# Three weight loads of a kernel's opening stage tied to later matmuls

## The chip, the cores and the metric

One Trainium2 chip, one NeuronCore. The metric is the device time of one launch in microseconds (us). Every kernel shown was run several times, and one further execution was taken by the hardware profiler. The engines are named as the profile names them: PE (matmul) with PEld (its weight loads into the array), ACT (ScalarE), DVE (VectorE), POOL (GpSimd) and SP (SyncE, which here does nothing but issue DMAs). A name with a q at its end (SPq, PEq) is the engine's sequencer, the part that reads instructions, waits on semaphores and issues DMAs.

## The reference

The first half is a recurrence over 768 time steps for 4 batches of 8 heads, each with a state of 48 x 48. The second is a two-layer network with h - tanh(h) between the layers.

```python
for t in range(S):
    cur = np.einsum('bhd,bhe->bhde', u[None] * kt, vt)
    y[:, :, t] = np.einsum('bhd,bhde->bhe', rt, state + cur)
    state = wt[:, :, :, None] * state + np.einsum('bhd,bhe->bhde', kt, vt)
...
x = y.transpose(0, 2, 1, 3).reshape(B * S, H * D)        # 3072 x 384
h = x @ w_in                                             # 3072 x 2048
out = (h - np.tanh(h)) @ w_out                           # 3072 x 384
```

## The kernel before

**Blocks.** Time is cut into 8 blocks of 384 tokens (4 batches, 2 halves of the sequence each). A block's recurrence is done in chunks of 64 steps. Within a chunk everything is a matmul: scores of keys against queries (`own` for the diagonal, `earlier` for what lies off the diagonal, both through `gram`, whose matmuls are line L488 of the profile), the chunk's addition to the state (`update_half`, L611), and the result from states (`from_states`, L673) and from scores (`from_scores`, L691). The result is the network's input xT, three tiles of 128 rows. Then 16 steps f follow in the main loop, one for each 128 columns of `w_in`: three products into one bank (L837), ACT's copy out of it (L840), the polynomial that stands for h - tanh(h), and the second product (L914, or L961 in later blocks). While one block is in the network, the recurrence of the next is done between its steps.

**The boot.** The first block has nothing to hide behind. `boot` writes its order out by hand: the block's heads go in two halves, h1 and h2. For h1: `own`, transposes of the keys (`turn_1`, L511), `earlier`, `update_half`, then `from_scores` and `from_states`. For h2: `update_half`, `own`, `earlier`, `from_states`, `from_scores`. Between these DVE runs the scans of the decays (L411, L423), the scans of the states (`states_half`, L627), and the masked copies of scores out of PSUM (`own()` and `earlier()`, L496). ACT copies the results out (`result_out`, L725), and small DMAs put the rows that lie in a tile of their own into the gaps of xT (`fill_holes`, L732; three on SP's queue, three on POOL's).

**The weights.** They come as 64-bit numbers and are turned into 32 bits on the chip. One `more_weights` issues one raw load (768 KB, line L249) on SP; `convert` makes three ACT pieces (L262: one writes `w_sb`, two write `up`) and one on DVE (L266) of it. There are 16 raw loads. In the order of their issue I number them raw 1, raw 2 and so on; raw 1 to raw 6 belong to the boot, and the main loop issues one in most of its first steps, each tied to ACT's copy of that step. Five buffers hold raw loads.

**Order.** PE, ACT, DVE and SP run in exactly the written order. SP issues one DMA after another, and a DMA that must wait holds up all that are written behind it. `begin_behind(ins, dma)` adds such a wait: the DMA is not issued before the instruction `ins` has ended. `self.done` is the last matmul that a block has written down so far; `self.opened` is the first matmul of the group that was begun last.

What the boot puts on SP's queue, in order: nine loads of the first block's inputs, raw 1, raw 2, a half of the next block's w, raw 3, three `fill_holes`, raw 4, the other half of w, raw 5, the next block's k, raw 6.

Of the kernel before, what the change touches and what calls it, by code (L numbers as in the profile page):

```python
# [125 lines left out]
def kernel(  # L126
# [12 lines left out]
    nc = tc.nc  # L139
# [106 lines left out]
    def load_weights(n, queue):  # L246
        raw = conv.tile([P, 2 * DM, 2], I32, name="raw", tag="raw")
        src = weights[UNITS[n]].bitcast(I32).rearrange("p (n two) -> p n two", two=2)
        return *UNITS[n], raw, queue.dma_start(out=raw, in_=src)  # L249

    def convert(part, j, raw, _, tiles=1):

        lo, hi = raw[:, :, 0], raw[:, :, 1]
        a = w_sb[:, part, 2 * j:2 * j + 2].rearrange("p f c -> p (f c)").bitcast(I32)
        up = conv.tile([P, 2 * DM], I32, name="up", tag="up", bufs=4)
        low, high = (up.bitcast(t).rearrange("p (n two) -> p n two", two=2)[:, :, i]
                     for i, t in enumerate((U16, F16)))

        def scaled(to, of, scale, bias=0.0):
            return lambda: nc.scalar.activation(out=to, in_=of, func=AF.Copy, scale=scale, bias=bias)  # L262

        return [scaled(a.bitcast(F32), hi.bitcast(F32), HIGH_SCALE), scaled(high, hi.bitcast(F32), SIGN_SCALE),
                scaled(low, lo.bitcast(U32), *LOW)], [
                lambda of=slice(i * 2 * DM // tiles, (i + 1) * 2 * DM // tiles): nc.vector.scalar_tensor_tensor(  # L266
                    out=a[:, of], in0=a[:, of], scalar=3, in1=up[:, of], op0=ALU.logical_shift_left,
                    op1=ALU.bitwise_or) for i in range(tiles)]
# [45 lines left out]
    class Block:  # L314
# [186 lines left out]
        def own(self, ps, p0, **fill):  # L501
            return self.masked(ps, "k", "r", masks["diagonal"], p0, **fill)

        def earlier(self, ps, p0, **fill):
            return self.masked(ps, "post", "pre", masks["above"], p0, **fill)
# [89 lines left out]

        def update_half(self, pair, p0):

            self.opened = None
            self.by_column = [t[:, 0:D * NCH].rearrange("d (e c) -> d e c", c=NCH) for t in pair]
            for x in range(UP):  # L600
                if x:
                    nc.tensor.drain().then_inc(fence, 1)
                    fences.append(None)
                    nc.tensor.wait_ge(fence, len(fences))
                for c in range(0, NCH, 2):
                    for h in range(2):
                        for par in range(2):
                            p = (x + par) % UP
                            toks = slice(64 * par, 64 * par + 64)
                            e0 = (p0 + p) * D2 + h * D  # L610
                            self.done = nc.tensor.matmul(self.by_column[p][64 * h:64 * h + 64, :, (c + par + 1) % NCH],  # L611
                                             lhsT=self.ks[toks, p0 + p, c // 2, 64 * h:64 * h + 64],
                                             rhs=self.v[toks, c // 2, e0:e0 + D], start=True, stop=True)
                            self.opened = self.opened or self.done

        def totals_by_column(self, p0):

# [449 lines left out]
    def more_weights(queue):  # L1067
        raws.append(load_weights(more_weights.n, queue))
        more_weights.n += 1
        return raws[-1][-1]  # L1070
# [3 lines left out]
    def begin_behind(ins, dma):  # L1074
        tc.add_manual_dep(dma.ins, ins.ins.name, mybir.DependencyInfo(
            mybir.DependencyClass.Sync, mybir.DependencyReason.DATA))

    def run(ops):
        for op in ops:
            op()  # L1080
# [13 lines left out]
    def boot(ps, pair, blk, later):  # L1094
        h1, h2 = HALVES
        blk.tiles["w"] = states0
        for name, p0, n in (("w", h1 + 1, 1), ("w", h1, 1), ("k", h1, UP), ("r", h1, UP), ("w", h2, UP)):
            blk.load(name, p0, n)
        blk.load_v(h1, UP)
        blk.load("k", h2, UP)  # L1100
        blk.load_v(h2, UP)
        blk.load("r", h2, UP)
        more_weights(nc.sync)

        both = (h1, h1 + 1), (h2, h2 + 1)
        blk.behind(h1 + 1, 1)
        blk.behind(h1, 1)
        blk.take_whole(h1, UP)
        blk.totals_by_column(h1)
        nc.scalar.copy(out=later_ident, in_=ident)  # L1110
        blk.before(h1, UP)
        blk.times_behind(h1, UP)
        blk.times_u(h1, UP)
        own = blk.own(ps, h1, spare=92, ahead=5, late=6)
        blk.turn_1(ps, h1)
        blk.times_before(h1, UP)
        earlier = blk.earlier(ps, h1)
        blk.behind(h2, UP)
        blk.take_whole(h2, UP)
        first_a, first_b = convert(*raws.pop(0), tiles=2)  # L1120
        own()
        blk.turn_2(h1)
        blk.totals_by_column(h2)
        blk.update_half(pair, h1)
        begin_behind(blk.opened, more_weights(nc.sync))
        later.load("w", UP, UP)
        blk.times_behind(h2, UP)
        blk.times_u(h2, UP)
        blk.turn_1(ps, h2)
        blk.turn_2(h2)  # L1130
        earlier()
        blk.results(ps, halved=True)
        blk.result("from_scores", both[0])
        run(blk.states_half(h1))
        blk.result("from_states", both[0], True)
        blk.before(h2, UP)
        blk.update_half(pair, h2)
        begin_behind(blk.opened, more_weights(nc.sync))
        blk.times_before(h2, UP)
        own = blk.own(ps, h2)  # L1140
        run(first_a[:1])
        blk.result_out((3,), nc.scalar.copy)
        blk.result_out((2,))
        earlier = blk.earlier(ps, h2)
        onwards = blk.states_half(h2)
        own()
        run(first_a[1:])
        blk.fill_holes([nc.sync, nc.gpsimd])
        more_weights(nc.sync)
        later.load("w", 0, UP)  # L1150
        second_a, second_b = convert(*raws.pop(0))
        third_a, third_b = convert(*raws.pop(0))
        run(second_a)
        more_weights(nc.sync)
        blk.results(ps, halved=True)
        blk.result("from_states", both[1])
        earlier(1, 1)
        earlier(0, 1)
        for p in reversed(both[1]):
            blk.result("from_scores", (p,), True, more=True)  # L1160
        blk.result_out((1,), nc.scalar.copy)
        later.load("k")
        more_weights(nc.sync)
        run(onwards)
        run(first_b[:1])
        blk.result_out((0,), nc.vector.tensor_copy)
        run(first_b[1:])
        run(third_a[:2])
        run(second_b)
        blk.held(0, NPAIR)  # L1170
        return [(third_a[2], third_b)]
# [6 lines left out]
    with tc.tile_pool(name="ps_boot", bufs=1, space=PSUM) as ps_boot:  # L1178
        pieces = boot(Turns([scratch(ps_boot)] + ps_a.both), [hp] + acc, blocks[0], blocks[1])
# [227 lines left out]
```

## Time and profile before

| | |
|---|---|
| median of 3 runs | 555.3 us |
| lowest, highest | 553.42, 555.8 us |
| the profiled execution's own time | 555.92 us |
| its span in the trace | 554.1 us |
| PE busy | 539.7 us, 97% of the span |
| DVE busy | 459.7 us, 83% |
| ACT busy | 405.0 us, 73% |

Times in the trace count from the first instruction; 1.8 us of the profiled execution lie outside the span. "Idle before" in a row is the time in which the engine did nothing ahead of that instruction, followed by what released it. "Issue" in the chain of waits is time in which an engine waited for nothing that the profile can show. In the DMA view, "q1" is SP's queue, and "instruction" rows are the queues through which engines get their own code.

### The profile page before, as it was taken

The page shows a single profiled execution, that of the slowest core. Times are in us where ns is not written, and L with a number is a line of the kernel's source. Part 1 is how long each engine was busy: PE and PEld are TensorE (multiplying, and loading weights), DVE is VectorE, ACT ScalarE, POOL GpSimd, SP SyncE. Part 2 cuts the span into 40 slices and gives each one's busy share as a digit, 9 for nine tenths or more (in the row PEclk, how much of TensorE's full clock was granted, in tenths as well). Part 3 has the DMA queues.
Part 4 walks back from the last instruction along what each step waited for, and adds up shares of the span by engine and source line. Part 5 has one row for each costly group of instructions (what it writes and reads, how often), then busy time and mean ns, then how long its engine had stood idle before and what let it go on. Part 6 is the DMA issues. An engine that isn't in the chain of part 4 may idle for free.

```text
span 554.1 us, 14163 instructions
## 1 busy us (share of the span) xinstructions
PE 539.7 (97%) x5727; PEld 405.1 (73%) x5727; DVE 459.7 (83%) x943; ACT 405.0 (73%) x814; POOL 5.3 (1%) x33
## 2 busy tenths in 40 slices
PE   8599999999999999999999999999999999999996
PEld 5565556678777787777778787777877787787874
DVE  7679999999988989888997889969797897557563
ACT  4589997798667886588766886588865886666561
POOL 1100000000000000000000000000000000000000
PEclk9789999999999999999999999999999999999999
DMA  8878654244302442237211532126232320100101
GB/s 274 281 258 317 206 178 126 72 122 95 117 13 85 101 117 84 69 79 143 98 54 44 144 116 64 50 88 157 61 93 62 80 65 3 54 1 0 44 2 46
DMA packets 53462, 56.31 MB, mean 102 GB/s; under 512 B 21520, under 2 KB 51344, under 8 KB 53392
## 3 DMA queue, kind: packets, MB, share of 16 engines
q1 hardware_dynamic: 53008, 55.18, 33.6%
q8 instruction: 46, 0.75, 0.6%
q14 instruction: 24, 0.20, 0.1%
q10 hardware_dynamic: 288, 0.10, 0.1%
q0 software_dynamic: 96, 0.07, 0.1%
HBM read 44.73 MB, written 4.72 MB: 89 GB/s over the span
## 4 chain that ended last, share of the span: by engine, by line
PE 90%; ACT 4%; issue 2%; DMA 1%; DVE 1%; PEld 0%; SPq 0%; PEldq 0%; DVEq 0%
PE hp L837 43%; PE acc L961 26%; PE att L961 6%; PE acc L914 4%; PE att L488 2%; ACT up L262 2%; PE att L691 2%; PE att L673 2%; PE acc L939 2%; PE att L569 1%; DMA states<-in_wT 1%; ACT w_sb L262 1%; ACT qa L869 1%; DVE scores L496 0%; ACT h L840 0%
## 5 line engine op out<-in xcount | busy, mean ns | idle before, releaser
L837 PE MATMUL hp<-xT,w_sb 128*128 128x384 f32 x750 | 265.5, 490 | 0.4 <-ACT h L840 0.4
L837 PEld LDWEIGHTS hp<-xT,w_sb 128*128 128x128 f32 x750 | 134.9, 192 | 72.3 <-ACT h L840 1.0
L840 ACT ACTIVATE h<-hp 128x384 f32<-128x384 f32 x125 | 61.5, 492 | 101.5 <-PE hp L837 101.4
L961 PE MATMUL acc<-forms,g 128*128 128x128 f32 x954 | 133.7, 276 | 0.5
L961 PEld LDWEIGHTS acc<-forms,g 128*128 128x128 f32 x954 | 121.6, 192 | 10.2 <-issue 1.2
L843 DVE SCALAR_TENSOR_TENSOR h<-h,s 128x384 f32<-128x384 f32 x128 | 70.9, 554 | 52.3 <-ACT s L858 52.1
L884 DVE TENSOR_TENSOR g<-g 128x256 f32<-128x256 f32 x265 | 103.6, 421 | 7.9 <-PE acc L961 7.0
L859 ACT ACTIVATE qa<-s,shift 128x384 f32<-128x384 f32 x113 | 69.8, 618 | 3.7
L861 ACT ACTIVATE junk<-s,shift 128x384 bf16<-128x384 f32 x113 | 68.0, 602 | 0.0
L843 DVE SCALAR_TENSOR_TENSOR g<-qa,h 128x384 f32<-128x384 f32 x112 | 61.8, 552 | 1.9 <-DVE h L843 0.5
L858 ACT ACTIVATE s<-h 128x384 f32<-128x384 f32 x113 | 59.3, 525 | 3.5
L961 PEld LDWEIGHTS acc<-w_sb,g 128*128 128x128 f32 x318 | 46.7, 191 | 9.7 <-ACT sums L929 0.3
L961 PE MATMUL acc<-w_sb,g 128*128 128x128 f32 x318 | 53.1, 276 | 0.1
L961 PE MATMUL att<-w_sb,g 128*128 128x128 f32 x212 | 35.5, 275 | 0.0
L961 PEld LDWEIGHTS att<-w_sb,g 128*128 128x128 f32 x212 | 31.1, 192 | 5.3
L996 DVE TENSOR_TENSOR sums<-sums 128x256 f32<-128x256 f32 x84 | 33.1, 410 | 1.7 <-ACT sums L973 1.4
L914 PE MATMUL acc<-w_sb,sums 128*128 128x384 f32 x96 | 33.9, 489 | 0.1
L262 ACT ACTIVATE up<-raw 128x768 f16<-128x768 f32 (+1 forms) x32 | 33.2, 1075 | 0.0
L914 PEld LDWEIGHTS acc<-w_sb,sums 128*128 128x128 f32 x96 | 17.8, 190 | 12.1 <-DVE sums L843 0.3
L411 DVE TENSOR_TENSOR_SCAN pre<-w,start 128x780 f32<-128x780 f32 x14 | 25.0, 1783 | 0.5
L423 DVE TENSOR_TENSOR_SCAN post<-w,seed 128x780 f32<-128x780 f32 x14 | 24.9, 1776 | 0.0
L861 ACT ACTIVATION_READ_ACCUMULATOR junk<-s,shift 128x1 f32 x113 | 21.3, 189 | 0.0
(115 smaller groups left out, 523.8 us busy)
## 6 DMA issues: line engine op xcount, KB each, us to landing
raw<-in_weights SPq DMA_DIRECT2D x16, 768.0 KB, 4.9
k<-in_kT SPq DMA_DIRECT2D x7, 768.0 KB, 4.4
r<-in_rT SPq DMA_DIRECT2D x7, 768.0 KB, 4.5
w<-in_wT SPq DMA_DIRECT2D x6, 780.0 KB, 4.6
v_sb<-in_v SPq DMA_DIRECT2D x7, 576.0 KB, 3.8
k<-in_tokens SPq DMA_DIRECT2D x7, 576.0 KB, 3.9
r<-in_tokens SPq DMA_DIRECT2D x7, 576.0 KB, 5.0
out_y<-sums SPq DMA_DIRECT2D x18, 128.0 KB, 1.9
```

The costliest lines, as they stand in the source:

```text
L262: return lambda: nc.scalar.activation(out=to, in_=of, func=AF.Copy, scale=scale, bias=bias)
L411: return nc.vector.tensor_tensor_scan(out=self.tile("pre")[:, cols], data0=self.tile("w")[:, cols], data1=start[:, 0:n * NCH * LP], initia ...
L837: nc.tensor.matmul(hp, lhsT=w_in_sb[:, f, kc, :], rhs=xT[kc], start=(kc == KC - 1), stop=(kc == 0))
L840: return h, nc.scalar.activation(out=h, in_=hp, func=AF.Copy, scale=1.0 / UPSCALE)
L843: return lambda: nc.vector.scalar_tensor_tensor(out=out, in0=in0, scalar=scalar, in1=in1, op0=op0, op1=ALU.mult)
L858: nc.scalar.activation(out=s, in_=h, func=AF.Square)
L859: nc.scalar.activation(out=qa, in_=s, func=AF.Square, bias=shift[:, 4:5])
L861: nc.scalar.activation(out=junk[:, 0:NB], in_=s, func=AF.Relu, bias=shift[:, 5:6], accum_out=excess[:, at:at + 1])
L884: return lambda: nc.vector.tensor_tensor(out=G[:, to:to + 2], in0=two(G, g_at(q, a0), g_at(q, a1)), in1=two(G, g_at(q, b0), g_at(q, b1)), ...
L914: nc.tensor.matmul(acc, lhsT=g[:, j * P:(j + 1) * P], rhs=w_out_sb[:, f, :], start=(f == self.first), stop=(f == NF - 1))
L961: nc.tensor.matmul(to, lhsT=G[:, g_at(q, a), :], rhs=rhs, start=start, stop=stop, skip_group_check=True)
L996: ops.append(lambda op=op, at=at: nc.vector.tensor_tensor(out=at[0], in0=at[1], in1=at[2], op=OPS[op]))
```

## The change

Raw 2 and raw 3 no longer wait for the first matmul of an `update_half` but for the last one. Raw 4, which waited for no matmul, now waits for the last matmul of the second half's off-diagonal scores. The bookkeeping of first matmuls in `update_half` goes. No instruction is added or taken away on any engine and none changes its place; three DMAs have other waits.

```diff
@@ update_half
-            self.opened = None
             self.by_column = [...]
...
                             self.done = nc.tensor.matmul(...)
-                            self.opened = self.opened or self.done
@@ boot
         blk.update_half(pair, h1)
-        begin_behind(blk.opened, more_weights(nc.sync))
+        begin_behind(blk.done, more_weights(nc.sync))
         later.load("w", UP, UP)
...
         blk.update_half(pair, h2)
-        begin_behind(blk.opened, more_weights(nc.sync))
+        begin_behind(blk.done, more_weights(nc.sync))
...
         earlier = blk.earlier(ps, h2)
+        scored = blk.done
         onwards = blk.states_half(h2)
         own()
         run(first_a[1:])
         blk.fill_holes([nc.sync, nc.gpsimd])
-        more_weights(nc.sync)
+        begin_behind(scored, more_weights(nc.sync))
         later.load("w", 0, UP)
```

## The prediction

> **What bounds the kernel now.** I read the page first, then the chain of waits over the boot's end, then SP's queue, the DMA packets in short stretches, and the stretches' busy times. From the page:
>
> ```profile
> PE 539.7 (97%) x5727; PEld 405.1 (73%) x5727; DVE 459.7 (83%) x943; ACT 405.0 (73%) x814; POOL 5.3 (1%) x33
> q8 instruction: 46, 0.75, 0.6%
> ```
>
> PE is busy nearly all the time, so the little it loses is worth asking for. The chain of waits shows where the boot loses it (start, length, what):
>
> ```profile
> 16.64 1.95 issue
> 18.59 0.13 PEld hp L611
> 20.03 2.15 PE att L488 x79
> 22.18 3.02 issue
> 25.20 0.75 PE att L488 x17
> 26.04 1.06 DVE scores L496 x2
> ...
> 28.99 4.15 PE hp L837 x6
> ```
>
> Twice PE waits for nothing visible, 1.95 us at the start of the second `update_half` and 3.02 us in the middle of the second `earlier`. The middle of a group has no wait of the program. Queue q8 gives a reading: 46 packets in 0.75 MB are 16 KB each, and PE's 2 x 5727 instructions over 46 are 249 a packet. So q8 is PE's code, in blocks of about 250 instructions. The stretches (busy us and instructions of PE, then of PEld, then of the others; further on the granted clock and the DMAs' busy share) bear it out:
>
> ```profile
> 12.42:18.50 6.08, 3.87 (x143) 3.15 (x135) 6.01 (x10) 4.57 (x9) 0.90 (x2) 1.00 0.66 241
> 18.55:25.00 6.45, 3.48 (x126) 3.19 (x127) 2.68 (x4) 4.26 (x5) 0.63 (x2) 0.57 0.83 259
> 16.04:19.45 3.41, 1.49 (x70) 1.24 (x66) 2.77 (x3) 2.71 (x6) 1.58 (x3) 1.00 0.40 138
> ```
>
> Between the stalls lie 126 + 127 = 253 instructions, one block; one block back from the first stall is about 12.4 us. Both stalls are PE waiting for its next code block. SP's queue and the DMA view say why the code was late. First SP's issues (start, length; the row from 5.72 is raw 1 with raw 2 merged in), then the code packets in the stretches 16.0 to 16.3, 22.8 to 22.9 and 28.8 to 28.9, then landings (us from issue) of raw 1, raw 2, raw 3, w, two fills on SP, raw 4 and raw 6:
>
> ```profile
> 5.72 7.17 SPq L249 DMA_DIRECT2D raw<-in_weights  x2
> ...
> 12.55 0.34 SPq L249 DMA_DIRECT2D raw<-in_weights  x1
> 12.94 0.43 SPq L363 DMA_DIRECT2D w<-in_wT  x1
> 18.88 0.33 SPq L249 DMA_DIRECT2D raw<-in_weights  x1
> 19.31 1.89 SPq L732 DMA_DIRECT2D xT<-late  x3
> 21.24 0.58 SPq L249 DMA_DIRECT2D raw<-in_weights  x1
> 24.21 0.48 SPq L249 DMA_DIRECT2D raw<-in_weights  x1
> ```
>
> ```profile
> q8 instruction: 1, 0.02, 19.4%
> q8 instruction: 1, 0.02, 58.3%
> q8 instruction: 1, 0.02, 62.2%
> ...
> raw<-in_weights SPq DMA_DIRECT2D x1, 768.0 KB, 9.5
> raw<-in_weights SPq DMA_DIRECT2D x1, 768.0 KB, 4.5
> raw<-in_weights SPq DMA_DIRECT2D x1, 768.0 KB, 5.0
> w<-in_wT SPq DMA_DIRECT2D x1, 390.0 KB, 6.3
> xT<-late SPq DMA_DIRECT2D x2, 24.0 KB, 5.3
> raw<-in_weights SPq DMA_DIRECT2D x1, 768.0 KB, 5.5
> raw<-in_weights SPq DMA_DIRECT2D x1, 768.0 KB, 9.4
> ```
>
> The first code packet begins after 16.0 and lasts 0.194 x 16 x 0.3 = 0.93 us; PE goes on at 18.59, about 1.4 us after it ends. The second begins after 22.8 and PE goes on at 25.20: again 0.93 and 1.4. If PE asks for a block when it enters the one before (at about 12.4 and at 18.59), the two requests waited almost 4 us. In both cases a 768 KB raw load left within 0.3 us of the request (raw 2 at 12.55, raw 3 at 18.88), and the code packet came shortly before that load landed: raw 2 lands at 12.55 + 4.5 = 17.05, raw 3 at 23.88, each about 0.9 us after the packet's start. My reading: the code stood behind the raw load that had just got in ahead of it.
>
> **The change, part by part.** It moves three issues and what SP holds behind them; on PE, ACT and DVE the order is the same. I follow the boot from 12.4 us.
>
> *Raw 2*, tied to the last matmul of the first update. What that adds is read from the second update: raw 3 left at 18.88, after its first matmul, and the chain's next row begins at 20.03, so the last matmul ends 1.15 us later. Raw 2 leaves at 12.55 + 1.15 = 13.7, w behind it at 14.1. Ahead of PE's request of 12.4 is then only raw 1, which landed at 5.72 + 9.5 = 15.2. With the same 0.9 us before the landing, the code packet starts by 14.3 and PE has its block by 14.3 + 0.93 + 1.4 = 16.6. It needs it at 16.64. So the first stall goes: 1.95 us, or, if the packet starts only when raw 1 has landed, 1.0. Raw 2's delay is hidden: it lands by 13.7 + 4.5 = 18.2, and ACT begins on it at 20.05 (row below).
>
> *Raw 3*, tied to the last matmul of the second update. That update now runs from 16.64 to 18.1 (1.44 us as before), and raw 3 leaves at 18.2, even earlier than its 18.88. PE's request for the block after falls at 16.64, 1.5 us ahead of it. Ahead of the request are raw 2 (lands 18.2) and w (14.1 + 6.3 = 20.4). If the packet goes in 0.9 us ahead of one or the other, it starts between 17.3 and 19.5, and PE has its code between 19.6 and 21.8; I take the middle, 20.7, as no row says which.
>
> PE and DVE then go on as follows:
>
> ```profile
> 9.43 1.08 PE L488 MATMUL att<-r,k 48*64 48x64 f32 x48
> 17.93 0.96 DVE L430 TENSOR_TENSOR pre<-r,pre 128x768 f32<-128x768 f32 x1
> 20.05 0.89 ACT L262 ACTIVATE w_sb<-raw 128x768 f32<-128x768 f32 x1
> 20.15 0.76 DVE L627 TENSOR_TENSOR_SCAN first_states<-hp,first_totals 128x288 f32<-128x288 f32 x1 [1.26 <-PE hp L611]
> 21.47 1.02 DVE L496 COPY_PREDICATED scores<-mask_all,att 128x768 f32<-128x768 uint8 x1
> 28.41 0.96 ACT L725 COPY xT<-att 48x384 f32<-48x384 f32 x2 [5.60 <-PE att L691]
> 30.19 1.06 ACT L262 ACTIVATE up<-raw 128x768 f16<-128x768 f32 x1
> 33.17 0.49 ACT L840 ACTIVATE h<-hp 128x384 f32<-128x384 f32 x1 [1.92 <-PE hp L837]
> 34.48 0.90 ACT L262 ACTIVATE w_sb<-raw 128x768 f32<-128x768 f32 x1
> 36.89 2.10 PE L837 MATMUL hp<-xT,w_sb 128*128 128x384 f32 x6
> 41.87 0.92 ACT L262 ACTIVATE w_sb<-raw 128x768 f32<-128x768 f32 x1
> ```
>
> `own` takes 1.08 us, 18.1 to 19.2. `earlier` may start then (DVE's pre is ready at 17.93 + 0.96 = 18.89, whatever PE does). Its first 31 matmuls (79 in the chain's row less the 48 of `own`) end at 19.9, and the code comes at 20.7: a stall of 0.8 us (0 to 1.9) in place of 3.02. `earlier` ends at 21.1. DVE meanwhile starts its two scans at 18.9 instead of 20.15; they and the first masked copy took until 21.47 + 1.02 = 22.49, so now until 21.2 or 21.3. Here DVE becomes what is late next. `from_states` writes the bank that this copy reads and starts at 21.3 instead of after 25.2. The second pair of copies (1.06) ends at 22.4, `from_states` too (48 matmuls, 1.08). `from_scores` ends at 23.5 against 28.99. That is 5.5 us.
>
> The first product hp took 4.15 us at half clock and takes 1.93 at full clock (36.89 and 2.10 with its last matmul's tail). It would end at 25.4, but xT must be copied first (ACT's 0.96 from the middle of `from_scores`, DVE's last copy about 1 us from its end), so 25.3 to 25.5, against 33.14. ACT has 31.25 - 28.41 = 2.84 us of work ahead of h: from 23.0 to 25.8. So h of step 0 starts at 25.9 at best instead of 33.17: 7.3 us. From this I take 0.6 for the fills: SP's three leave at 18.5 to 20.4 behind raw 3, and at 5.3 us the last are there at 25, not at 23.5. **Sum 6.7 us.** From there ACT and PE are both almost gapless, and the main loop moves forward as a whole.
>
> *Raw 4*, tied to the end of `earlier`, at 21.1. Before it left at 21.24, so it is no later, but on its queue wait the other w, raw 5, k and raw 6. ACT needs raw 4 at 34.48 - 6.7 = 27.8; it lands at 21.1 + 5.5 = 26.6. Raw 6 left at 24.21 and lands after 9.4 us; moved with raw 4 it is there at 33.5, due at 41.87 - 6.7 = 35.2. Raw 4's cover is 1.2 us, raw 6's 1.7. If `earlier` ends at 22.2, the upper bound, raw 4's is 0.1, and beyond that every us costs one. PE's block after that is asked for ahead of raw 4.
>
> *The clock.* In the stretch 16.04 to 19.45 PE was busy 1.49 of 3.41 us, and the clock fell to one half right after (0.57 in the row from 18.55) and stayed there through hp. With the first stall gone this stretch is full. The stretch after holds 0.8 + 0.2 us of gaps ahead of `from_states`, up to 1.9 with the bounds, so more work than the one that lost the clock. If the clock falls there, hp runs at 4.15 and its end moves to 27.5, that of step 1 by up to 2 more: the gain is 6.7 - 2 = 4.7 us. The Trainium skill, TensorE: Matmul & The Clock Gate (Part 1: The HAM clock gate), has the clock halved after an idle window of about 3.4 us; by that rule a stretch with work in it would keep it, and only the 6.7 stands. The trace disagrees in degree: 1.49 us of work did not keep it.
>
> So the profiled execution goes from 555.92 to 549.2, and the median, 0.6 lower, from 555.3 to 548.6; I say **549.0**.
>
> **The rivals.** *Half clock*, above: 4.7 us, 550.6. For it speaks that the clock falls on stretches only half empty; against it the first stall's going.
>
> *The code isn't held by the raw loads.* The Trainium skill, DMA: Bandwidth & Descriptors (Queues, rings and completion order), has each DMA engine take turns between queues packet by packet; then a code block would wait for one data packet, not for a load, and reordering loads would move nothing. In rows: the packet at 28.8 to 28.9 went out while raw 6 (lands 33.6) was still queued, so a queue does not have to be empty. Then the second stall stays and at most the first one's 1.95 goes: 553.4 to 555.3, no measurable difference. Against it: two waits of almost 4 us that end 0.9 us ahead of a raw load's landing.
>
> *Loads too late.* With compute earlier by 6.7, the loads of raw 4 to raw 6, w, k and the loop's own raw loads crowd into one stretch, all behind raw 4's new wait. It decides from the point where raw 4 lands after 27.8 and raw 6 after 35.2. For a loss, raw 6 must land past 41.87, at least 17.7 us after an issue at 24.1 and nearly twice its 9.4. If the wait holds SP that long, 3 to 4 us are lost: 559. Nothing in the rows shows such a landing.
>
> **How the numbers follow.** Full clock 0.50, half clock 0.27, code not held by the loads 0.13, loads too late 0.10. Measurement can tell about 0.5%, 2.8 us, from no change; 552.5 is the line. So faster 0.77, same 0.13, slower 0.10. The gaining cases reach from 547.5 (h at its best, 7.3 us, and 0.5 of spread) to 552; the range goes on to 555.5 to hold most of the third case.
>
> **What would show it.** In the profile after: the two issue waits (1.95 and 3.02) gone and at most some 1 us left in `earlier`; code packets near 14 and 18 us; raw 2 at 13.7, raw 3 near 18.2, raw 4 near 21; `from_scores` over near 23.5; h of step 0 near 26; no new wait of ACT for raw. I am wrong if the stalls stay with raw 2 and raw 3 behind the requests, or if ACT's idle time ahead of L262 grows.

## The result, and the profile after

| | before | after |
|---|---|---|
| median of 22 runs each | 554.73 us | 551.25 us |
| lowest, highest | 549.31, 556.25 us | 549.6, 552.58 us |
| the profiled execution's own time | 555.92 us | 551.86 us |
| its span in the trace | 554.1 us | 550.1 us |

The ratio after to before is 0.9942, with a 95% interval of 0.9927 to 0.9958. The change makes the kernel 3.5 us faster by the medians and 4.06 us by the two profiled executions. The prediction had 549.0, so it forecast 6.3 us. The lowest execution of the kernel before, 549.31, lies below all of the kernel after; "What stays open" comes back to it.

The page of the kernel after. PE is still the engine that is busy nearly all the time:

```profile
span 550.1 us, 14164 instructions
PE 536.6 (98%) x5727; PEld 403.5 (73%) x5727; DVE 459.4 (84%) x943; ACT 403.9 (73%) x814; POOL 5.2 (1%) x33
```

The chain of waits of the kernel after over the boot's end (start, length, what):

```profile
17.65 0.97 DVE pre L430
18.62 0.14 issue
18.75 0.69 PE att L488 x31
19.44 2.85 issue
22.29 0.75 PE att L488 x17
...
23.12 1.06 DVE scores L496 x2
...
24.54 1.53 PE att L689 x48
26.08 3.11 PE hp L835 x6
```

The reader is to see two things. The stall of 1.95 us at the second `update_half` is gone: the chain runs through DVE's `pre` into `earlier` instead. The stall in the middle of `earlier` is still there, behind the same 31 matmuls as predicted, and it is 2.85 us long where it was 3.02.

SP's queue in the kernel after (start, length of each group of issues). The first row is raw 1 with raw 2 merged in; it ends at 13.73, so raw 2 itself left at 13.4. The rows from 17.59 and 23.06 are raw 3 and raw 4:

```profile
5.66 8.07 SPq L249 DMA_DIRECT2D raw<-in_weights  x2
13.78 1.30 SPq L363 DMA_DIRECT2D w<-in_wT  x1
17.59 0.33 SPq L249 DMA_DIRECT2D raw<-in_weights  x1
18.07 2.02 SPq L730 DMA_DIRECT2D xT<-late  x3
23.06 0.33 SPq L249 DMA_DIRECT2D raw<-in_weights  x1
```

The code packets in the DMA view of the kernel after, first in the stretch 13.7 to 13.9, then in 19.8 to 19.9 (packets, MB, busy share of 16 engines):

```profile
q8 instruction: 1, 0.02, 29.0%
q8 instruction: 1, 0.02, 64.4%
```

The first block of code now begins to come at 13.8 instead of 16.3, though raw 2 left 0.4 us before it. The second comes at 19.8 and lasts 0.644 x 16 x 0.1 = 1.03 us; PE goes on at 22.29, again 1.4 us after its end. PE entered the block before it at about 16.2, so from entry to packet it is 3.6 us.

The stretches of the kernel after (PE's, PEld's, DVE's, ACT's, POOL's busy us, then granted clock, DMA share, GB/s):

```profile
17.76:21.17 3.41, 1.18 (x66) 0.94 (x56) 3.07 (x4) 3.41 (x5) 1.15 (x3) 1.00 0.84 265
21.17:24.58 3.41, 2.02 (x69) 1.84 (x69) 1.46 (x5) 1.33 (x2) 0.13 (x2) 0.50 0.45 112
24.58:27.99 3.41, 3.41 (x51) 2.45 (x52) 2.11 (x5) 2.46 (x4) 0.00 (x0) 0.50 0.91 341
27.99:31.40 3.41, 3.41 (x12) 2.03 (x11) 2.11 (x5) 2.53 (x5) 0.00 (x0) 1.00 1.00 391
```

The clock still falls to one half right behind the stretch with the stall. It stays there for two stretches of 3.41 us, from 21.17 to 28.0; before, it was four of them, from 19.45 to 33.1. And ACT's row for h of step 0 in the kernel after:

```profile
29.21 0.49 ACT L838 ACTIVATE h<-hp 128x384 f32<-128x384 f32 x1 [0.88 <-PE hp L835]
```

It began at 33.17 before: 3.96 us earlier. The span is 4.0 us shorter, so the main loop moved forward as a whole and nothing was given back later.

### The profile page after: what moved, and what is told of

Same layout as the page of the kernel before. It is cut to its first block, busy times and chain, and to the rows that moved or that the text cites. A ratio compares the mean times of both kernels' runs of the same rounds, so it can differ in the third digit from the quotient of the medians.

```text
span 550.1 us, 14164 instructions
## 1 busy us (share of the span) xinstructions
PE 536.6 (98%) x5727; PEld 403.5 (73%) x5727; DVE 459.4 (84%) x943; ACT 403.9 (73%) x814; POOL 5.2 (1%) x33
## 4 chain that ended last, share of the span: by engine, by line
PE 90%; ACT 4%; DVE 2%; issue 1%; DMA 1%; SPq 0%; DVEq 0%
PE hp L835 43%; PE acc L959 26%; PE att L959 6%; PE acc L912 4%; ACT up L262 2%; PE att L488 2%; PE att L689 2%; PE att L671 2%; PE acc L937 2%; PE att L569 2%; DMA r<-in_rT 1%; ACT w_sb L262 1%; ACT qa L867 1%; ACT h L838 0%; DVE pre L430 0%
## 5 line engine op out<-in xcount | busy, mean ns | idle before, releaser
L859 ACT ACTIVATION_READ_ACCUMULATOR junk<-s,shift 128x1 f32 x113 | 21.1, 187 | 0.0
```

The source lines that it names most:

```text
L859: nc.scalar.activation(out=junk[:, 0:NB], in_=s, func=AF.Relu, bias=shift[:, 5:6], accum_out=excess[:, at:at + 1])
```

## The experiments

The theory by which the prediction stood, the queue: a code block waits behind the raw loads that are queued when PE asks for it, so the right order of loads removes both stalls. The first rival: the code isn't held by loads at all. The second, formed after the first four runs: a code block has a time of its own that no order of loads shortens (the floor), and a load that gets ahead adds to it. Ratios are against the kernel before on the same chip, with 95% intervals.

**Raw 2 alone.** Only the first of the three edits, made to the kernel before:

```diff
         blk.update_half(pair, h1)
-        begin_behind(blk.opened, more_weights(nc.sync))
+        begin_behind(blk.done, more_weights(nc.sync))
```

> Only raw 2 is moved to the last matmul of the first update; raw 3 and raw 4 leave as in the kernel before. Theory A (a code block stands behind the loads queued when PE asks for it) and theory B (a code block waits as long as the DMA engines have any loads to do, also loads issued after the request): the first stall (1.95 us) goes in both. PE then asks for the next block at 16.2, with raw 2 and w under way and raw 3 leaving at about 16.5, so the second stall stays at 2.8 to 3.5 us in both. Time about 1.9 us below before plus up to 1.5 if the clock also keeps its pace longer: 551 to 553. Theory C (the loads do not hold the code): both stalls as before, 554.7.

Measured: median 553.56 (549.02 to 555.08), ratio 0.9985 [0.9958, 1.0012]. Its profiled execution, 550.66, was the second fastest of twelve and so not a typical one. In it the first stall is gone and the second is 1.18 us, by its chain of waits:

```profile
18.81 0.69 PE att L488 x31
19.49 1.18 issue
20.68 0.75 PE att L488 x17
...
24.47 3.46 PE hp L837 x6
```

So raw 2's edit does take the first stall away, which speaks against the first rival. The medians show no gain that is clear of noise. Ten of the twelve executions took 552.38 us or more; where they lost what this one kept, no trace shows. The second stall is what both theories of the expectation had wrong, at 2.8 to 3.5 us: raw 3 left at 16.65, 0.4 us behind PE's entry at about 16.3, and the code packet still came at 18.33 and not near 20. And the DMA engines weren't idle meanwhile (the DMA share is the last number but one):

```profile
16.83:20.24 3.41, 2.04 (x108) 1.73 (x104) 3.38 (x5) 3.36 (x6) 1.57 (x3) 1.00 0.99 356
```

**Raw 3 and raw 4 alone.** The other two edits, made to the kernel before (raw 2 stays tied to the first matmul):

```diff
         blk.update_half(pair, h2)
-        begin_behind(blk.opened, more_weights(nc.sync))
+        begin_behind(blk.done, more_weights(nc.sync))
...
-        more_weights(nc.sync)
+        begin_behind(scored, more_weights(nc.sync))
```

> Only raw 3 and raw 4 are moved, raw 2 leaves as before. A and B: the first stall stays at 1.95 us; PE asks for the next block at 18.6, when raw 2 and w have landed or nearly so and raw 3 has not left (it goes at 20), so the code packet comes by 19.5 and the second stall is 0 to 0.5 us in place of 3.02. Time about 2.5 to 3 us below before: 551.5 to 552.5. C: both stalls stay, raw 4 leaves at 26, time 554.7 or a little above.

Measured: 552.71 (550.61 to 553.83), ratio 0.9969 [0.994, 0.9997]. Its chain of waits:

```profile
16.47 1.92 issue
18.40 0.13 PEld hp L611
...
19.62 1.75 PE att L488 x79
21.38 1.35 issue
22.73 0.75 PE att L488 x17
...
26.52 4.00 PE hp L837 x6
```

The first stall stays, as it should. The second is not gone, as expected at 0 to 0.5 us, but more than halved, 1.35 us. PE entered the block at 18.40 and raw 3 left only at 19.68; the code packet came at 20.2. Something other than a raw load took those 1.8 us: the DMA engines were busy for 0.18 of them.

**Raw 3 far later.** Raw 3 behind the fills and tied to `earlier`, with raw 4 right behind it, to keep it away from the second code block altogether:

```diff
         blk.update_half(pair, h2)
-        begin_behind(blk.done, more_weights(nc.sync))
...
         begin_behind(scored, more_weights(nc.sync))
+        more_weights(nc.sync)
```

> The changed kernel with raw 3 issued behind the fills, tied to the end of the off-diagonal scores, with raw 4 right behind it. In the changed kernel PE asks for the second block at 16.2, raw 2 and w are queued, raw 3 leaves at 17.59, and the code packet starts at 19.84. A: the request is older than raw 3, so nothing changes: packet at 19.5 to 19.9, stall 2.5 to 2.9 us, time as the changed kernel, 3.5 below before. B: the packet goes in when w's data are through, at 18.5 to 18.9, stall 1.5 to 1.9 us, time 1 us below the changed kernel (4.5 below before), unless raw 3 is then late for ACT.

Measured: 551.29 (550.62 to 551.8), ratio 0.9948 [0.9926, 0.997]. The code packet came at 18.45, the stall is 1.19 us, the clock stays at 1.0 and hp takes 2.29 us; but raw 3, issued at 21.36, is now what ACT waits for. Its waits and ACT's row:

```profile
ACT w_sb L262 <- DMA raw<-in_weights: 2.5, 2, 1.7
```

```profile
27.73 0.49 ACT L838 ACTIVATE h<-hp 128x384 f32<-128x384 f32 x1
```

What PE gained was lost to the load: h at 27.73, and no better median than the changed kernel's.

**The half of w later.** The changed kernel with the first half of w moved from behind raw 2 to behind raw 4, so that only raw 2 is on its way when PE asks for the second block:

```diff
-        later.load("w", UP, UP)
...
         begin_behind(scored, more_weights(nc.sync))
+        later.load("w", UP, UP)
         later.load("w", 0, UP)
```

> The changed kernel with the first half of the next block's w issued beside the second half, behind raw 4, instead of right behind raw 2. Ahead of PE's request of 16.2 is then only raw 2, whose data end at about 17.3, and raw 3 leaves at 17.6. A: packet at 17.0 to 17.4, second stall 0 to 0.4 us. B: the same if the gap between raw 2's end and raw 3's first data at 18.4 lets it in, packet at 17.3 to 18, stall 0.2 to 1. Both: time 2 to 2.8 us below the changed kernel, that is 5.5 to 6.3 below before. C: stall 2.85 us as in the changed kernel, no difference from it.

Measured: 550.16 (548.78 to 551.62), ratio 0.9929 [0.9903, 0.9954]. PE's waits, the row of hp and ACT's row of h in its trace:

```profile
PE att L488 <- issue: 0.9, 1, 0.9
PE hp L835 <- DMA xT<-late: 0.6, 1, 0.6
```

```profile
23.93 2.17 PE L835 MATMUL hp<-xT,w_sb 128*128 128x384 f32 x6 [0.57 <-DMA xT<-late]
26.14 0.49 ACT L838 ACTIVATE h<-hp 128x384 f32<-128x384 f32 x1 [0.19 <-PE hp L835]
```

This is the chain that the prediction drew: a stall of 0.9 us in `earlier`, full clock, h at 26.1, its own time 549.12. Between 17.6 and 18.2 the DMA engines moved nothing (0.1% by the DMA view) and the code packet still came only at 18.23. With only raw 2 ahead, the queue theory would have had the code there by 17.4.

**All loads late.** To measure the code's own time, raw 2 goes behind the second `update_half`, raw 3 and raw 4 behind `earlier`, w behind both:

```diff
         blk.update_half(pair, h1)
-        begin_behind(blk.done, more_weights(nc.sync))
-        later.load("w", UP, UP)
...
         begin_behind(scored, more_weights(nc.sync))
+        more_weights(nc.sync)
+        later.load("w", UP, UP)
```

> A probe for the code's latency, not for speed: raw 2 only behind the second update (17.6), raw 3 and raw 4 behind the off-diagonal scores, w behind them, so that the DMA engines have nothing to do from about 14 to 18.5, and PE asks for the second block at 16.2 to 16.4. R: packet 1.9 us after that, at 18.1 to 18.4, stall 0.9 to 1.3 although nothing was queued. B (a block waits only as long as there are loads): packet at about 17.0, no stall. In both ACT waits for raw 2 from about 20 to 22.5, so h of the first step starts at about 28 to 29 and the time is near the changed kernel's or up to 2 us above.

Measured: 552.39 (550.9 to 553.31), ratio 0.9949 [0.9934, 0.9964], with ACT waiting 2.8 us for a raw load. What it was run for, first a stretch with its DMA share, then the code packet in 18.1 to 18.3, then PE's waits:

```profile
14.00:17.60 3.60, 3.20 (x154) 2.80 (x156) 3.57 (x7) 2.90 (x6) 0.24 (x1) 1.00 0.01 3
```

```profile
q8 instruction: 1, 0.02, 42.3%
```

```profile
PE att L488 <- issue: 1.5, 1, 1.5
```

The DMA engines had stood all but still (share 0.01) for over two us when PE entered the block at about 16.3, and the packet came only at 18.17. So about 1.9 us lie between entry and packet with nothing in the way. The packet took 1.35 us in this trace; with the 0.9 that it takes in most, and some 1.4 until PE goes on, the sum is 4.2 us. PE runs through the block in 3.0 to 3.1 us (16.2 to 19.3 in the kernel after, of which 0.5 is a wait for DVE's `pre`). No order of loads tried here brought this stall below 0.86 us. The queue theory falls in this part.

But 1.9 us is what this block shows, not a time that every block needs. At the block before it, which PE enters at about 12.4, the packet came 0.7 us after the entry with raw 2 alone (at 13.16) and 1.5 us after it with all loads late (at 13.9), and at the block behind it 1.1 us after PE went on with the half of w later (20.47 to 21.60). So the floor is measured for this block alone, and why it differs from its neighbours stays open.

**Raw 2 and raw 3 without raw 4.** The changed kernel without the third edit:

```diff
-        begin_behind(scored, more_weights(nc.sync))
+        more_weights(nc.sync)
```

> The changed kernel without its third edit: raw 4 leaves right behind the fills again. First stall gone, second as in the changed kernel (about 2.9 us, packet at 19.8), since raw 4 would leave at about 20.1, after that packet. Theory D (the tie of raw 4 is needed to keep the code ahead of it): a longer second stall, 3.5 us or more, and 0.5 to 1 us above the changed kernel. Theory E (the tie of raw 4 matters for nothing): time equal to the changed kernel, ratio to before 0.993 to 0.996.

Measured: 551.39 (549.84 to 553.33), ratio 0.9942 [0.9922, 0.9963], the same as with it. The third edit makes no difference that these runs can measure. Up to raw 4 this kernel orders everything as the changed one does, yet in its profiled execution raw 3 left at 18.00, the packet came at 18.4, and the stall was 0.86 us, the shortest of all:

```profile
20.70 0.47 PE L488 MATMUL att<-pre,post 48*64 48x64 f32 x17 [0.86 <-issue]
```

The same order can go either way.

**Raw 3 behind `own`.** Raw 3 tied to the last matmul of the second `own`, some 1.2 us later:

```diff
-        begin_behind(blk.done, more_weights(nc.sync))
         blk.times_before(h2, UP)
         own = blk.own(ps, h2)
+        begin_behind(blk.done, more_weights(nc.sync))
```

> The changed kernel with raw 3 tied to the last matmul of the second half's own scores, about 1 us later than to the update's last. Theory R (race with a floor): a code packet starts at the earliest about 1.9 us after PE has entered the block before, and a load whose data reach the engines by then goes first; raw 3 at 17.59 was in time for that in the changed kernel (packet 19.84) and is not at 18.7. Then packet at 18.2 to 18.5, stall 0.9 to 1.3 us in place of 2.85, and raw 3 lands at about 23.5, in time for ACT at 24: time 1 to 2.5 us below the changed kernel, 5 to 6 below before, with the half-clock windows rarer. Theory A (the block stands behind raw 2 and w, which were queued at its request): packet still near 19.8, stall 2.5 to 2.9, no gain on the changed kernel.

Measured: 551.39 (550.18 to 551.66), ratio 0.9931 [0.9911, 0.9952]. In the trace the stall is 1.48 us and the packet is at 18.95, half a us later than expected. The clock is at one half from 21.06 to 27.89, and hp takes 3.51 us. h is at 28.71, only half a us ahead of the changed kernel's.

**Both of these.** The half of w later and raw 3 behind `own`, the two edits above together:

> raw 3 behind the own scores and also w beside its other half behind raw 4. R: the floor stays, packet at 18.2 to 18.5, stall 0.9 to 1.3, the same as with raw 3 moved alone; time the same as that or 0.5 us above, since raw 5 is later by a w. A: with only raw 2 ahead the packet comes at 17.0 to 17.4, stall 0 to 0.3, 1 us below raw 3 moved alone.

Measured: 550.11 (548.91 to 551.45), ratio 0.9911 [0.9889, 0.9934], the lowest of all kernels here, though by less than the noise. Its profiled execution (551.45, its slowest) had a stall of 1.48 us and half clock over hp, 4.18 us.

**Sixteen more instructions.** The changed kernel with eight more spare matmuls (with their weight loads) at the start of the boot. If the stall stands at the border of a code block it must move back by eight matmuls; if it belongs to the step, it must not:

```diff
-        own = blk.own(ps, h1, spare=92, ahead=5, late=6)
+        own = blk.own(ps, h1, spare=100, ahead=5, late=6)
```

> The changed kernel with 8 more of the tiny matmuls that PE does at the start (16 more instructions ahead of everything else). If the second stall is a border between code blocks (theory R), it comes exactly 16 instructions, 8 matmuls, earlier in the off-diagonal scores: the chain shows L488 x23 before and x25 after it instead of x31 and x17 (some 23 to 25 each; the trace may miss a record). Time within 0.3 us of the changed kernel. If the stall belongs to a place in the program (a wait that the profile doesn't show), it stays at x31 and x17.

Measured: 550.99 (548.86 to 553.22), ratio 0.9929 [0.9899, 0.9959]. Its chain of waits:

```profile
18.86 0.57 PE att L488 x23
19.43 2.94 issue
22.37 0.90 PE att L488 x25
```

The stall stands after 23 matmuls of `earlier` instead of 31 and has its old length. It belongs to the instruction count. That was argued in the prediction from packet sizes; here it is shown. The packet in this trace began at 19.0, 0.9 us ahead of the changed kernel's, but took 2.05 us instead of 0.9 to 1.0. That the loads beside it stretched it is likely, not shown.

**The fills ahead of raw 3.** The changed kernel with raw 3, tied to `own`, put behind SP's three fills; and the same with the half of w later:

```diff
-        begin_behind(blk.done, more_weights(nc.sync))
         blk.times_before(h2, UP)
         own = blk.own(ps, h2)
+        owned = blk.done
...
         blk.fill_holes([nc.sync, nc.gpsimd])
+        begin_behind(owned, more_weights(nc.sync))
```

> The changed kernel with raw 3 behind SP's fills and behind the own scores, at about 20. R: code packet at 18.2 to 18.4, stall 1.1 to 1.5; the fills are not behind raw 3 any more; raw 3 lands at about 24.5, so ACT waits for it 0.3 to 0.8 us. Time 0 to 1 us below the changed kernel. If what is left is the half clock after the stall and not the loads, time follows the number of half-clock windows: 549.5 to 550 with one or none, 551.5 with three.

> The same with w beside its other half behind raw 4. R: stall 1.1 to 1.5 as well; raw 3 lands at 24 to 24.5, raw 4 and raw 5 behind it in time. Time as the kernel with w late and raw 3 at 17.7 (550.2) or up to 1 us below, 549 to 550.2, about 1 us below the changed kernel.

Measured: 551.03 (549.99 to 551.79), ratio 0.9927 [0.9903, 0.9951]; and with w later 550.53 (550.11 to 550.75), ratio 0.9918 [0.9889, 0.9947]. The chain of waits of the first:

```profile
19.57 1.46 issue
21.02 0.51 PE att L488 x17
...
24.54 4.12 PE hp L835 x6
```

and its stretch with half clock:

```profile
21.66:28.48 6.82, 6.55 (x96) 4.41 (x92) 4.39 (x10) 3.85 (x6) 0.11 (x2) 0.50 0.95 357
```

The packet came at 18.7 and raw 3 left at 20.75. The stall is half as long, and hp one us longer than in the changed kernel. Of the 1.39 us that the stall gives, 0.53 reach h (28.68 against 29.21). In the second kernel the stall is 0.93 us, and ACT waits 1.9 us for a raw load that left at 20.2.

**The changed kernel once more**, unchanged, to see its stall in a second profiled execution:

> The changed kernel as it is, one more look. Theory R (a race): the same program can win or lose the race between raw 3 and the code packet from one execution to the next. So either packet at 18.2 to 18.6 with a second stall of 1.1 to 1.6 us (won), or packet at 19.6 to 20 and 2.7 to 3.0 us (lost); in both the first stall stays away, and the time is 549.5 to 552.6. Theory A: always packet near 19.8 and 2.9 us.

Measured: one time, 552.64. The kernel before ran once beside it and took 548.67 at a granted clock of 1.0, 4 us less. One execution of each says nothing of the medians, but this is the shortest execution on record here, so the kernel before can run without its loss. The changed kernel's chain of waits:

```profile
18.83 0.69 PE att L488 x31
19.52 2.85 issue
22.37 0.76 PE att L488 x17
...
26.16 3.66 PE hp L835 x6
```

Raw 3 left at 17.85, the packet came at 19.86, and the stall is 2.85 us as in the first trace. With the kernel without the third edit, whose order is the same up to there, that is two late packets in three traces.

## Why the prediction was right, and where it was off

**Faster, and inside the range: right.** For the first stall the cause was the one named, a code block that came late behind a raw load: in the two traces in which raw 2 left at 12.5 the packet began at 16.3 and 16.1, in the twelve in which it left at 13.4 or later, at 13.2 to 13.9. The shift by eight matmuls shows that the second stall stands at a border between blocks too. That a raw load held that block is shown only in part: it came late with raw 3 at 17.59 and 17.85, but in time with raw 3 at 16.65.

**Raw 2: right.** It left at 13.4 (predicted 13.7), the packet came at 13.8 (by 14.3), and PE ran on through the second `update_half`. Its 1.95 us went as predicted and nothing waited for the load. The margin was small: with the packet's 0.93 us and some 1.4 more the block was there at 16.1, and PE needed it at 16.2. In the second trace of the changed kernel, with the packet at 13.9, PE's weight loads still paused there, from 16.23 to 16.56.

**Raw 3: the step that failed.** It left at 17.59 (predicted 18.2), but the code came at 22.29, not 20.7. The step took the packet to be waiting for raw 2 or w and put it at the middle of two landings, 17.3 to 19.5. What the runs showed in its place: this block's packet came no sooner than 18.17 in any trace, 1.9 us after PE's entry even with idle DMA engines, and at 19.8 to 19.9 in both traces of the changed kernel. The stall was 2.85 us instead of 0.8, outside the bounds given for it, 0 to 1.9. Of the 2.05 us, 0.45 are PE's earlier arrival (19.44, predicted 19.9); PE went on 1.6 us later than forecast.

**DVE next, and the order behind: right, but mis-sized.** The steps followed as drawn once the code was there, but from there to the end of `from_scores` they took 3.8 us (22.29 to 26.08) and not 2.8 (20.7 to 23.5). The last 17 matmuls took 0.75 us for 0.4 and `from_scores` 1.53 for 1.1, both with the clock at one half (0.51 and 0.89 at full clock, with raw 3 far later), and the forecast left out DVE's `states`, 0.27 us ahead of `from_scores`. In the kernel with w later, where the stall is 0.9 us, h began at 26.1, where the prediction had 25.9 and up to 0.6 for the fills. There PE waited 0.57 us for a fill; in the changed kernel PE has no wait for a fill.

**The clock: the second rival held here, at a smaller price.** Half clock (4.7 us, 550.6, chance 0.27) was the case that came nearest. The stretch from 17.76 holds 1.18 us of PE work in 3.41, and the clock fell. It came back at 28.0, so that hp took 3.11 us, not 4.15, against the 1.93 of the forecast: 1.2 us. The Trainium skill, TensorE: Matmul & The Clock Gate (Part 1: The HAM clock gate), would have kept full clock, as the stretch was not idle; the trace doesn't agree, as it did not before.

**The sum.** 6.7 less 1.6 for the later code, less 1.0 from there to the end of `from_scores`, less 1.2 for hp, plus the 0.5 that was set aside for ACT's work ahead of h and the 0.6 for the fills, is 4.0. Measured are 3.96 at h and 4.06 for the execution. So three steps took 3.8 us more than forecast, and 1.1 us that had been set aside and weren't needed made part of that good; that part is luck.

**Raw 4: right.** It cost nothing and brought nothing. It left at 23.06 instead of 21.1, as `earlier` ended later; in the stretch from 15 to 32 us PE and ACT have no wait for a raw load.

**The code isn't held by loads: fell for the first block.** The stalls themselves came out as this rival had them, the first gone and the second nearly whole (2.85 of 3.02 us); the time fell further, by the 1.04 us among others that hp won as the clock came back sooner. The Trainium skill, DMA: Bandwidth & Descriptors (Queues, rings and completion order), has engines take turns packet by packet. The first stall's going and 19.8 against 18.2 for the packet don't agree with a wait for a single packet. But the rival was right in one thing: part of the wait is not the loads' doing. And with raw 2 alone the code came at 18.33 between DMA engines that were busy 0.99 of the time, so busy engines alone do not hold it. The Trainium skill, Runtime: NRT & Kernel Launch (Instruction fetch mechanics), calls the cost of the border between two blocks mostly hidden; here this block takes 4.2 us to come and 3.1 to run, and 1 us shows.

**How the three edits share the gain.** Raw 2 alone gives 0.9985 [0.9958, 1.0012], raw 3 with raw 4 gives 0.9969 [0.994, 0.9997], raw 2 with raw 3 gives 0.9942, the same as all. The product of the first two, 0.9954, lies inside the intervals of both kernels that have raw 2 and raw 3 moved, so the runs do not show that the edits need each other. That the clock takes part of what one edit gives while the other stall stays is argued from the traces, not shown by a run of its own. The 22 runs of the changed kernel go with the clock: the nine with a granted clock of 0.997 or more have a median of 550.22 us, the thirteen with 0.991 to 0.994 have 551.79. Since a longer stall may also cost the clock, the 1.57 us between them are not the clock's alone.

**What stays open.** What decides whether the packet comes at 18.2 to 18.4 or at 19.8. Raw 3's time of issue alone doesn't: it left at 17.59 and 17.85 with late packets, at 18.00 and, with raw 2 alone, at 16.65 with early ones. Full DMA engines don't either, as the row of raw 2 alone shows. And why the kernel before ran under 550 us in 5 of its 93 executions on record (548.67 to 549.79), four of them with a clock on record, 0.996 to 1.0: no trace of such an execution was kept, so whether its stalls were short there or only the clock stayed is not known. Nor did any run show where the clock's limit lies. Stretches with 1.18 and 1.49 us of PE work in 3.41 lost it, and so did the one with 2.04 in the row of raw 2 alone; this one of the kernel with w later, with 2.00 in 3.50, kept it:

```profile
17.00:20.50 3.50, 2.00 (x107) 1.76 (x108) 3.47 (x5) 3.45 (x6) 1.57 (x3) 1.00 0.53 156
```

In these traces the clock changes on a grid of 3.41 us, which lies differently in each execution. Counted on from its first change, at 6.51 us, that trace's own stretch runs from 16.75 to 20.16 and holds 2.17 us. With the fills ahead of raw 3 and w later, a stretch with 2.23 us (19.24 to 22.65) lost the clock, so PE's busy time alone doesn't decide it. The stall's length doesn't decide it alone either: 1.19 us kept the clock in the kernel with raw 3 far later, 1.18 us lost it in the one with raw 2 alone.

**A better version.** With the half of w later the median is 550.16, and with raw 3 behind `own` as well 550.11. Against the kernel before on the same chip that is 0.7 and 1.7 us more than the changed kernel's gain, by the ratios. Their intervals overlap with its own, so that they beat it is likely, not shown; both beat the kernel before.

## What to carry to other kernels

A gap of "issue" in the middle of a group of matmuls, some 250 instructions after the last one, was a wait for code here: shift the instruction stream by a few and see whether the gap moves. A load that is issued just after PE entered a block of small matmuls can hold up the next block, as raw 2 did at 12.55, so it is worth trying large loads behind the code packet; it doesn't always do so, as raw 3 at 16.65 showed, and one trace of each order is too few to tell. Where the block runs in less time than its successor takes to come, the order of loads can't close the rest. And when a stall goes away, read the granted clock in the stretches behind it before counting the gain, for the clock can take back much of it.

## What the runs showed of the hardware

One block of PE's code took about 1.9 us from PE's entry into the block before to the first byte with DMA engines that stood still (16.3 to 18.17), 0.9 to 1.35 us to move, and some 1.4 us more until PE went on. I had expected the packet at once when the queue is empty. From entry to first byte the block before took 0.7 us with raw 2 alone (from 12.4), and the block behind took 1.1 us with the half of w later (20.47 to 21.60).

The time of a code packet varied too: 2.05 us instead of 0.9 in the kernel with eight more matmuls.

The granted clock fell after stretches that held 1.18 to 2.23 us of PE work in 3.41, kept full speed after one with 2.17 (the half of w later), and stayed at one half for one to four such stretches. With the fills ahead of raw 3, a stall of 1.46 us cost two of them, as many as the stall of 2.85 us in the changed kernel.
